# A ring of six tiles with loads of three tiles in a one-core attention decode kernel

## The chip, the core and the metric

The kernel runs on one core of one Trainium2 chip. The metric is the device time of one execution, in microseconds. Five engines matter here: TensorE (PE; its weight loads are shown apart as PEld), VectorE (DVE), ScalarE (ACT), GpSimd (POOL), and SyncE (SP), which in this kernel only issues DMAs, one after the other. The transfers themselves run on 16 DMA engines. "Clock" is the share of its full speed that TensorE was granted.

## The reference

One decode step for four sequences (B = 4, D = 512): adaptive layer norm, attention over a cache with 32 query heads and 8 key/value heads of 4096 keys and 128 channels, and a mixer block over one token. All is fp32.

```python
mod = (silu(c) @ w_mod).reshape(4, 6, 1, -1)
sa, ca, ga, sb, cb, gb = (mod[:, t] for t in range(6))
h = layernorm(x) * (1 + ca) + sa
q = (h @ wq) in 32 heads;  k, v = the caches, each shared by 4 query heads
o = softmax(q k^T * 128 ** -0.5) v
x = x + ga * (o @ wo)
h = layernorm(x) * (1 + cb) + sb
x = x + gb * (gelu(layernorm(h) outer w1 + b1) @ w2 + b2)      # 1792 hidden units
```

The caches are 2 x 32 blocks (4 sequences by 8 heads) of 2 MB each, 128 MB or so of the 157 MB that are read.

## The kernel before

A "head" below is one of the 32 pairs of a sequence and a key/value head, numbered i = 0 to 31 (`NS` = 32). Its keys are a tile of 128 channels by 4096 keys (16 KB in each of 128 partitions), its values one of the same size.

**Buffers.** `ring` has three buffers of 32 KB in each partition, 96 KB in all. A buffer holds two tiles. First it takes the modulation terms 0 and 1 (`wm01`) and the query weights in two halves, then the keys of heads 0 and 1 (`load_first`), then, load by load, K(i+2) and V(i) (`load_pair(i)`), which lie next to each other in HBM, so that one DMA has 128 rows of 32 KB. A buffer is taken again when both of its tiles were read. The modulation terms 2 to 4 (`load_wm24`) pass through a ring buffer too. The output weights, 64 KB in each partition, have tiles of their own (`wo_p`), filled by four DMAs of two heads each (`load_wo`).

**Order.** The program's order is each engine's order (a manual schedule): an engine does its instructions in turn and waits at semaphores. SP holds all loads, so a load that waits for its buffer holds back those behind it.

**A head's work**, in iteration i of the main loop (i = 0 to 23): `scores(i+2)` on PE (L231), the maximum of the scores (DVE, PE), the exponential (ACT, L261), the transposition of the probabilities of head i+1 (DVE, L267), `project(i-1)` with the output weights (PE, L343), and `values(i)` in two halves (PE, L291). So scores run two heads ahead of values. From i = 8 on, a `Mixer` runs beside it for the sequence that is finished: its normalisation, 14 hidden columns (DVE expands, ACT's gelu, PE contracts) and its sum, spread over eight iterations. Behind iteration 2, PE, ACT and DVE work out the modulation terms 2 to 4 (`mod`, L215 and L221).

**The last eight heads** follow an order that is written out (`PLAN`): s is scores, v values, t a transposition, p a projection, x, g and c the mixer's three steps, and LP, LT, LK, LV and LW are loads. The keys of heads 30 and 31 and the values of heads 28 to 31 are loaded on their own, the last values in small pieces, then modulation term 5. Behind the last values comes a serial end: the last projection, the last mixer and the output.

Of the kernel before, what the change touches and what calls it, by code (L numbers as in the profile page):

```python
# [18 lines left out]
P = 128  # L19
# [4 lines left out]
WIDE = {NS - 5: 24, NS - 4: 32}  # L24
NARROW = NS - 3


@with_exitstack
def adaln_decode(ctx: ExitStack, tc: tile.TileContext, small, x, wmod, wq, kk, kv, vv, wo, out):
# [17 lines left out]
    xr = wk.tile([P, D], F32, name="xr", tag="yw", bufs=1)[0:B]  # L47
    wm01 = ring.tile([P, 2, 4, D], F32, name="wm01", tag="kv")
    nc.sync.dma_start(wm01, wmod[0])
    nc.sync.dma_start(sm, small)  # L50
    nc.sync.dma_start(xr, x)
    wqt = []
    for k in range(0, 4, 2):
        t = ring.tile([P, 2, HQ * DH], F32, name=f"wq{k}", tag="kv")
        nc.sync.dma_start(t, wq[k // 2])
        wqt += [t[:, 0], t[:, 1]]
    w1, b1, w2 = sm[:, 0:NF], sm[:, NF:2 * NF], sm[:, 2 * NF:3 * NF]
# [32 lines left out]
    dv.memset(hT, 0.0)  # L90
    wo_p = [wos.tile([P, 2, REP, D], F32, name=f"wo{h}") for h in range(0, HKV, 2)]
    wo_t = [wo_p[h // 2][:, h % 2] for h in range(HKV)]
    prep = cst.tile([P, 4, P], F32, name="prep")
# [62 lines left out]

    KT, VT, WM = {}, {}, {}

    def slots():
        return ring.tile([P, 2, SK], F32, name="kv", tag="kv")  # L160

    def key(t, i):
        KT[i] = t

    def value(t, i):
        VT[i] = t.rearrange("p (j d) -> p j d", d=DH)

    def load_first():
        t = slots()
        nc.sync.dma_start(t, kk)  # L170
        key(t[:, 0], 0)
        key(t[:, 1], 1)

    def load_pair(i):
        t = slots()
        nc.sync.dma_start(t, kv[i])
        key(t[:, 0], i + 2)
        value(t[:, 1], i)

    def load_wo(h):  # L180
        nc.sync.dma_start(wo_p[h // 2], wo[h // 2])

    def load_wm24():
        w = ring.tile([P, 3, 4, D], F32, name="wm24", tag="kv")
        nc.sync.dma_start(w[:, 0:2], wmod[1])
        nc.sync.dma_start(w[:, 2], wmod[2][:, 0])
        for e in range(3):
            WM[2 + e] = w[:, e]

    def load_wm5():  # L190
        t = slots().rearrange("p s (k n) -> p (s k) n", n=D)
        nc.sync.dma_start(t[:, 0:4], wmod[2][:, 1])
        WM[5] = t[:, 0:4]
        return t[:, 4:6]

    def load_key(t, i):
        nc.sync.dma_start(t, kv[i - 2][:, 0])
        key(t, i)

    def load_v(t, i, cuts):  # L200
        value(t, i)
        src = (kv[i][:, 1] if i < NS - 2 else vv[i - NS + 2]).rearrange("p (j d) -> p j d", d=DH)
        for lo, hi in zip(cuts, cuts[1:]):
            nc.sync.dma_start(VT[i][:, lo:hi], src[:, lo:hi])

# [20 lines left out]
    def scores(i):  # L226
        b, h = divmod(i, HKV)
        S[i] = s = ps_s.tile([P, 1024], F32, name=f"s{i}", tag="s")
        for n in range(2):
            for c in range(4):  # L230
                mm(s[32 * c:32 * c + 32, n * 512:(n + 1) * 512], QT[:, b, h, :],  # L231
                   KT[i][:, (n * 4 + c) * 512:(n * 4 + c + 1) * 512], start=True, stop=True)

    def row_max(i):
# [50 lines left out]
    def values(i, ks):  # L285
        if ks[0] == 0:
            PV[i] = ps_v.tile([P, 4 * DH], F32, name="pv", tag="pv")
        pT = PL[i][0]
        for k in ks:
            q = k % 4  # L290
            mm(PV[i][32 * q:32 * q + 32, :], pT[:, 128 * k:128 * k + 128:4],  # L291
               VT[i][:, 4 * k:4 * k + 4, :].rearrange("p j d -> p (j d)"), start=(k < 4), stop=(k >= 4))

    def values_narrow(i, ks, pv=None):
        if ks[0] == 0:
            PV[i] = ps_v.tile([P, DH], F32, name="pvn", tag="pv") if pv is None else pv
        pv = PV[i]
        pT = PL[i][0].rearrange("p (k r) -> p k r", r=32)
        top = 32 if i < NS - 1 else 30
        for k in ks:  # L300
            for j in range(4 * k, min(4 * k + 4, top)):
                c = j % 4
                mm(pv[32 * c:32 * c + 32, :], pT[:, j, :], VT[i][:, j, :], start=(k == 0), stop=(j + 4 >= top))  # L303

    def values_turned(i):
# [31 lines left out]
    def project(i, pa=None, between=None):  # L337
        b, h = divmod(i, HKV)
        oT = OT[i]
        if pa is None:  # L340
            pa = ps_m.tile([P, D], F32, name="pa", tag="m")
            for g in range(REP):
                mm(pa[32 * g:32 * g + 32, :], oT[:, g:g + 1].to_broadcast([P, 32]), wo_t[h][:, g, :],  # L343
                   start=True, stop=True)
        else:
            for g in range(REP):
                for c in range(4):
                    mm(pa[32 * c:32 * c + 32, :], oT[:, g:g + 1].to_broadcast([P, 32]),  # L348
                       wo_t[h][:, g, c * P:(c + 1) * P], start=(g == 0 and h == HKV - 2),
                       stop=(g == REP - 1 and h == HKV - 1))  # L350
                if between and g == 1:
                    between()
# [199 lines left out]
    def finish(b, pg, py, hb, wr):  # L552
        uu = ring.tile([P, 16, D], F32, name="uu", tag="kv")
        for js in ((0,), (1,), (2, 3, 4), (5, 6, 7), (8, 9, 10), (11, 12), (13,)):
# [34 lines left out]
    def fold_gate(gate, es):  # L589
        for e in es:  # L590
            w = wo_t[HKV - 2 + e // REP][:, e % REP]
            dv.tensor_tensor_reduce(w, w, gate, 1.0, 0.0, OP.mult, OP.add, rowsum[:, e:e + 1])
# [15 lines left out]

    load_first()
    load_pair(0)  # L610
    load_wo(0)
    for i in range(2):
# [5 lines left out]
    for i in range(NS - HKV):  # L618
        load_pair(i + 1)
        if i in (1, 3, 5):  # L620
            load_wo(i + 1)
        if i == 1:
            load_wm24()
        scores(i + 2)
# [22 lines left out]
        if mix:  # L647
            mix.outer(i % HKV)
        if i == 2:
            for t in range(2, 5):  # L650
# [4 lines left out]
                else:  # L655
                    nc.scalar.activation(dst, pm, AF.Copy)
        if i == NS - HKV - 2:
            gate = spread_gate()
# [3 lines left out]
    mix, row = Mixer(B - 2), Mixer(B - 1)  # L662
    pve = pgx = pc = ep = spare = slot = None
    gates = list(range(2 * REP))
    cuts = {NS - 1: (0, 16, 24, 28, 30, 32), NS - 2: (0, 16, 32)}
# [3 lines left out]
    x LP27 m26 S27 P24 m27 X26 X27 b26 B26 e26 x b27 v25.1 c g t26.1 l25 t26.0 B27 s28 V25 c g L25  # L669
    v26.0 v26.1 S28 x l26 f a25 L26 V26 A25 x m28 p25 LT X28 e27 c a26 P25 t27.0 A26 b28 s29 f B28 p26 e28  # L670
    LK30 t27.1 S29 P26 v27.0 m29 l27 g LK31 T t28.1 X29 LT t28.0 s30 L27 S30 b29 v27.1 B29 e29 l28 m30 V27
    LV28 L28 a27 g X30 t29.1 t29.0 l29 L29 s31 A27 LV29 b30 p27 x B30 S31 c c m31 e30 P27 X31 v28.0 f LT LV30
    b31 v28.1 B31 f e31 LV31 l30 V28 L30 t30.1 l31 L31 a28 t31.1 A28 p28 v29.0 v29.1 t30.0 f P28 V29 v30.0 a29
    v30.1 A29 LW p29 f v30.2 v30.3 t31.0 P29 g V30 Y y a30 A30 p30 E x v31.0 f v31.1 v31.2 v31.3 V31 z31 a31 I A31 j p31
    g T2 zs za zx zq c c zm zb0 T3 zv zb1 zw0 zn zc
    """
    TABLE = {"s": scores, "S": row_max, "m": turn_max, "X": col_max, "b": spread_max, "B": copy_max, "e": expo,
             "l": sums, "L": scale, "V": copy_v, "a": pick, "A": copy_o, "P": add_up,
             "LP": load_pair}
    MIX = {"F": mix.fold, "R": mix.residual, "G": mix.gather, "M": mix.modulate, "H": mix.gather, "Q": mix.spread,  # L680
# [3 lines left out]
    for step in PLAN.split():  # L684
# [17 lines left out]
        elif op == "p":  # L702
            project(i, pgx[:, 4] if i >= NS - 2 else None, mean_last if i == NS - 1 else None)
        elif op == "LT":
            slot = slots()
        elif op == "LK":
            load_key(slot[:, i % 2], i)
        elif op == "LV":
            load_v(slot[:, i % 2], i, cuts.get(i, (0, 32)))
        elif op == "LW":  # L710
            spare = load_wm5()
        elif op == "x":
            mix.expand(spare if mix.n == 6 else None)
        elif op == "f":
# [74 lines left out]
```

## Time and profile before

| | |
|---|---|
| three runs | 386.31, 386.43 and 390.96 us, median 386.43 |
| profiled execution | span 384.7 us from its first to its last instruction; the page gives no other time of it, and the median of the runs is 1.7 us longer |
| PE, DVE, ACT busy | 78%, 52%, 29% of the span |
| DMA | 7409 packets, 157.69 MB, 410 GB/s over the span |
| mean granted clock | 0.883 |

The span is measured on the core from first to last instruction; the device time also holds what lies around it. A row of the chain of waits gives the share of the span in which an engine, or a DMA, was what the end waited for. A row of instructions has line, engine, operation, output, inputs, shapes and count, then the start and the time; what stands in square brackets is the idle time ahead and what ended it. A window row has the busy times of PE, PEld, DVE, ACT and POOL, then the granted clock, the mean busy share of the DMA engines (which can pass 1 a little, by rounding at the window's edges) and GB/s.

### The profile page before, as it was taken

The page shows a single profiled execution, that of the slowest core. Times are in us where ns is not written, and L with a number is a line of the kernel's source. Part 1 is how long each engine was busy: PE and PEld are TensorE (multiplying, and loading weights), DVE is VectorE, ACT ScalarE, POOL GpSimd, SP SyncE. Part 2 cuts the span into 40 slices and gives each one's busy share as a digit, 9 for nine tenths or more (in the row PEclk, how much of TensorE's full clock was granted, in tenths as well). Part 3 has the DMA queues.
Part 4 walks back from the last instruction along what each step waited for, and adds up shares of the span by engine and source line. Part 5 has one row for each costly group of instructions (what it writes and reads, how often), then busy time and mean ns, then how long its engine had stood idle before and what let it go on. Part 6 is the DMA issues. An engine that isn't in the chain of part 4 may idle for free.

```text
span 384.7 us, 5604 instructions
## 1 busy us (share of the span) xinstructions
PE 298.7 (78%) x2380; PEld 117.2 (30%) x2380; DVE 198.2 (52%) x407; ACT 112.2 (29%) x144; POOL 7.7 (2%) x33
## 2 busy tenths in 40 slices
PE   0856777866966949979877878788888887999984
PEld 0112122311323313334322222342222343333653
DVE  1130251620451424664866545557665567778757
ACT  1001111121110110212567311124575105657276
POOL 1100000000000000000000000000000000000000
PEclk9989555985695685998999998999999999999999
DMA  8999999999999999999999999999999999999930
GB/s 331 433 433 436 411 453 433 409 432 436 423 441 433 434 436 436 434 436 431 429 425 433 428 433 434 429 433 431 429 434 436 434 436 432 424 417 423 418 122 3
DMA packets 7409, 157.69 MB, mean 410 GB/s; under 512 B 964, under 2 KB 1236, under 8 KB 1496
## 3 DMA queue, kind: packets, MB, share of 16 engines
q1 hardware_dynamic: 7376, 157.33, 95.4%
q8 instruction: 18, 0.29, 0.3%
q14 instruction: 7, 0.06, 0.0%
q10 hardware_dynamic: 8, 0.00, 0.0%
HBM read 157.32 MB, written 0.01 MB: 409 GB/s over the span
## 4 chain that ended last, share of the span: by engine, by line
DMA 60%; PE 29%; DVE 7%; ACT 2%; issue 1%; POOL 0%; SPq 0%; POOLq 0%; DVEq 0%
DMA kv<-in_kv 58%; PE s L231 8%; PE pv L291 7%; PE s L122 2%; PE qs L138 2%; DVE m L236 2%; DVE p L267 2%; DMA sm<-in_small 2%; PE pa L343 2%; PE pt L328 2%; ACT uu L562 1%; PE pb L251 1%; PE pve L303 1%; PE pm L240 1%; PE pgx L348 1%
## 5 line engine op out<-in xcount | busy, mean ns | idle before, releaser
L231 PE MATMUL s<-kv,QT 128*32 128x512 f32 x512 | 75.2, 714 | 38.9 <-DMA kv<-in_kv 37.0
L236 DVE TENSOR_REDUCE m<-s 128x1 f32<-128x1024 f32 x32 | 39.2, 1224 | 96.0 <-PE s L231 95.9
L261 ACT ACTIVATE p<-s,nm 128x1024 f32<-128x1024 f32 x32 | 35.7, 1115 | 180.6 <-DVE nm L256 180.5
L291 PE MATMUL pv<-kv,p 128*32 128x512 f32 x464 | 69.8, 670 | 0.7 <-DMA kv<-in_kv 0.7
L231 PEld LDWEIGHTS s<-kv,QT 128*32 128x32 f32 x512 | 15.8, 123 | 84.0 <-DMA kv<-in_kv 52.5
L328 PEld LDWEIGHTS pt<-g,po 128*128 128x128 f32 x236 | 31.1, 205 | 27.2 <-issue 19.9
L343 PE MATMUL pa<-wo,oT 128*32 128x512 f32 x240 | 34.6, 648 | 4.6 <-DVE oT L335 4.4
L328 PE MATMUL pt<-g,po 128*128 128x4 f32 (+2 forms) x236 | 33.9, 267 | 1.5 <-DVE po L314 1.0
L267 DVE STREAM_TRANSPOSE p<-p 128x1024 f32<-128x1024 f32 x25 | 30.9, 1234 | 0.0
L314 DVE COPY po<-pv 128x512 f32<-128x512 f32 x29 | 20.0, 688 | 16.8 <-PE pv L291 16.7
L245 DVE TENSOR_REDUCE mx<-pm 1x128 f32<-1x512 f32 x32 | 21.3, 669 | 1.1 <-PE pm L240 1.1
L442 DVE TENSOR_SCALAR u<-hb,wr,sm 128x512 f32<-128x512 f32 x40 | 19.9, 541 | 1.9 <-POOL wr L437 1.0
L506 ACT ACTIVATE u<-u 128x1024 f32<-128x1024 f32 x20 | 20.4, 1051 | 1.5 <-DVE u L442 1.4
L361 DVE TENSOR_TENSOR acc<-acc,pa 128x512 f32<-128x512 f32 x26 | 17.8, 686 | 4.3 <-PE pa L343 4.2
L261 ACT ACT_TABLE_LOAD x11 | 14.1, 1283 | 20.3 <-DVE nm L256 20.2
L251 PEld LDWEIGHTS pb<-neg,mx 1*128 1x128 f32 x64 | 10.4, 202 | 28.2 <-DVE mx L245 26.5
L122 PE MATMUL s<-wm,sT 128*4 128x512 f32 x16 | 9.1, 732 | 10.6 <-DVE sT L108 10.6
L506 ACT ACT_TABLE_LOAD x13 | 16.7, 1283 | 0.2
L291 PEld LDWEIGHTS pv<-kv,p 128*32 128x32 f32 x464 | 13.4, 146 | 7.2 <-issue 3.1
L240 PE MATMUL pm<-ident,m 128*1 128x128 f32 x32 | 9.3, 289 | 7.4 <-DVE m L236 3.5
L251 PE MATMUL pb<-neg,mx 1*128 1x1 f32 x64 | 13.1, 271 | 2.1 <-DVE mx L245 2.1
L453 PE MATMUL py<-u,sm 128*32 128x512 f32 x80 | 14.4, 616 | 0.0
(158 smaller groups left out, 214.7 us busy)
## 6 DMA issues: line engine op xcount, KB each, us to landing
kv<-in_kv SPq DMA_DIRECT2D x28, 4096.0 KB, 21.9
wq<-in_wq SPq DMA_DIRECT2D x2, 4096.0 KB, 16.3
wo<-in_wo SPq DMA_DIRECT2D x4, 2048.0 KB
kv<-in_kv SPq DMA_DIRECT2D x4, 2048.0 KB, 20.3
wm<-in_wmod SPq DMA_DIRECT2D x2, 2048.0 KB, 14.8
kv<-in_kk SPq DMA_DIRECT2D x1, 4096.0 KB
kv<-in_vv SPq DMA_DIRECT2D x3, 1024.0 KB
wm<-in_wmod SPq DMA_DIRECT2D x1, 1024.0 KB
```

The source lines that it names most:

```text
L231: mm(s[32 * c:32 * c + 32, n * 512:(n + 1) * 512], QT[:, b, h, :], KT[i][:, (n * 4 + c) * 512:(n * 4 + c + 1) * 512], start=True, stop=True)
L236: dv.tensor_reduce(M[i], S[i], axis=AX.X, op=OP.max)
L245: dv.tensor_reduce(mx, M[i].rearrange("o (c r) -> o r c", c=4).unsqueeze(1).to_broadcast([1, 4, 32, 4]), axis=AX.X, op=OP.max)
L251: mm(pb, M[i].rearrange("o c r -> o (c r)"), neg1, start=True, stop=True)
L261: nc.scalar.activation(p, S[i], AF.Exp, bias=M.pop(i), accum_out=l)
L267: dv.transpose(PL[i][0], PL[i][0])
L291: mm(PV[i][32 * q:32 * q + 32, :], pT[:, 128 * k:128 * k + 128:4], VT[i][:, 4 * k:4 * k + 4, :].rearrange("p j d -> p (j d)"), start=(k < ...
L314: dv.tensor_copy(PV[i], pv)
L328: mm(pt, po[:, c * DH:(c + 1) * DH], sel.unsqueeze(1).to_broadcast([P, m, REP]), start=(c == 0), stop=(c == n - 1))
L343: mm(pa[32 * g:32 * g + 32, :], oT[:, g:g + 1].to_broadcast([P, 32]), wo_t[h][:, g, :], start=True, stop=True)
L442: dv.tensor_scalar(u[:, e, :], hb, wr[:, j:j + 1], b1[:, j:j + 1], op0=OP.mult, op1=OP.add)
L506: nc.scalar.activation(u, u, AF.Gelu_apprx_tanh)
```

## The change

- The ring is one tile `RING` of six key or value tiles, again 96 KB in each partition. A list (`queue`) says what is loaded in which order, and `advance` issues the next loads as soon as the tiles that they overwrite have been read in the program's order. It is called behind `scores` and `values`.
- For heads up to 21, a load has three tiles, in rows of 48 KB: K(m+2), V(m), K(m+3), then V(m+1), K(m+4), V(m+2), and so on, 14 loads in all; the host lays the caches out so (`kvk`). Heads after that come in pairs, and the last ones alone, as before; the LP, LT, LK, LV and LW steps of `PLAN` are gone, and its other steps stand as they were.
- Output weights come in two DMAs of four heads. Modulation terms 0 and 1 land in the part of the output weights' tile for heads 0 and 1, and terms 2 to 4, in one DMA, in that for heads 4 to 6, so neither passes through the ring. The output weights are issued when these terms were read.
- The modulation terms 2 to 4 are worked out behind iteration 1, not 2.
- The buffers of the last mixer's hidden columns (`uu`) and of one expansion lie in fixed parts of `RING`.

```diff
-    ring = ctx.enter_context(tc.tile_pool(name="ring", bufs=3))
+    ring = ctx.enter_context(tc.tile_pool(name="ring", bufs=1))
...
+    RING = ring.tile([P, 6, SK], F32, name="kv")
+    wo_t = wos.tile([P, HKV, REP, D], F32, name="wo")
+    wm01, wm24 = wo_t[:, 0:2], wo_t[:, 4:7]
...
+    held, read = [("Q", 0), ("Q", 0), ("Q", 1), ("Q", 1), None, None], {None, ("Q", 0), ("Q", 1)}
...
+    def queue():
+        q = [entry(["K0", "K1"], kk)]
+        for n in range(NT):
+            m = n // 2 * 3
+            names = [f"V{m + 1}", f"K{m + 4}", f"V{m + 2}"] if n % 2 else [f"K{m + 2}", f"V{m}", f"K{m + 3}"]
+            q.append(entry(names, kvk[n]))
+        for i in range(NP, NS - 4):
+            q.append(entry([f"K{i + 2}", f"V{i}"], kv[i - NP]))
...
+        q.append(entry(["W5"], wm5))
+        q.insert(2, ("wo", "M0", wo_t[:, 0:4], wo[0]))
+        q.insert(4, ("wo", None, wm24, wm2))
+        q.insert(6, ("wo", "M2", wo_t[:, 4:8], wo[1]))
+        return q
+
+    LOADS, at = queue(), [4]
+
+    def advance(name=None):
+        read.add(name)
+        while LOADS:
+            kind, names, *rest = LOADS[0]
+            if kind == "wo":
+                if names not in read:
+                    return
+                nc.sync.dma_start(*rest)
+            else:
+                n, p = len(names), at[0]
+                if any(h not in read for h in held[p:p + n]):
+                    return
...
+                held[p:p + n] = names
+                at[0] = (p + n) % 6
...
+                elif len(names) > 1:
+                    nc.sync.dma_start(RING[:, p:p + n], rest[0])
...
+            LOADS.pop(0)
...
     def scores(i):
...
+        advance(f"K{i}")
...
-        if i == 2:
+        if i == 1:
             for t in range(2, 5):
...
+            advance("M2")
...
-    a23 v24.0 A23 p23 t25.0 P23 F R v24.1 LP25 G s26 t25.1 M H V24 LP26 Q a24 S26 v25.0 N s27 x A24 f p24 g
+    a23 v24.0 A23 p23 t25.0 P23 F R v24.1 G s26 t25.1 M H V24 Q a24 S26 v25.0 N s27 x A24 f p24 g
```

SP's loads from the keys of heads 0 and 1 on, before (`in_kk` and `in_kv` are the caches, `in_wo` the output weights, `in_wmod` the modulation terms; a size is partitions by fp32 elements):

```order
L170 DMA kv<-in_kk 128x8192
L176 DMA kv<-in_kv 128x8192
L181 DMA wo_128<-in_wo 128x4096
L176 DMA kv<-in_kv 128x8192 x2
L181 DMA wo_129<-in_wo 128x4096
L185 DMA wm_337<-in_wmod 128x4096
L186 DMA wm_337<-in_wmod 128x2048
L176 DMA kv<-in_kv 128x8192 x2
L181 DMA wo_130<-in_wo 128x4096
L176 DMA kv<-in_kv 128x8192 x2
L181 DMA wo_131<-in_wo 128x4096
L176 DMA kv<-in_kv 128x8192 x21
```

and of the change (`in_kvk` are the loads of three tiles, `in_wm` the modulation terms):

```order
L210 DMA kv<-in_kk 128x8192
L210 DMA kv<-in_kvk 128x12288
L192 DMA wo<-in_wo 128x8192
L210 DMA kv<-in_kvk 128x12288
L192 DMA wo<-in_wm 128x6144
L210 DMA kv<-in_kvk 128x12288
L192 DMA wo<-in_wo 128x8192
L210 DMA kv<-in_kvk 128x12288 x11
L210 DMA kv<-in_kv 128x8192 x7
```

Two big loads of output weights stand where four stood, both among the first six loads, and the second of them stands behind the modulation terms that it overwrites, with all further loads behind it.

PE's work around the modulation terms 2 to 4, before; the rows begin with the second half of head 2's values:

```order
L291 MATMUL pv<-kv,p 32x512 x4
L215 MATMUL pm_445<-wm_337,sT_134 32x512 x4
L221 MATMUL pc_452<-ym,g_122 32x128 x4
L215 MATMUL pm_458<-wm_337,sT_134 32x512 x4
L221 MATMUL pc_465<-ym,g_122 32x128 x4
L215 MATMUL pm_471<-wm_337,sT_134 32x512 x4
L221 MATMUL pc_478<-ym,g_122 32x128 x4
L231 MATMUL s_487<-kv,QT 32x512 x8
```

and of the change, where the rows begin with the second half of head 1's values:

```order
L306 MATMUL pv<-kv,p 32x512 x4
L229 MATMUL pm_380<-wo,sT_129 32x512 x4
L235 MATMUL pc_387<-ym,g_121 32x128 x4
L229 MATMUL pm_393<-wo,sT_129 32x512 x4
L235 MATMUL pc_400<-ym,g_121 32x128 x4
L229 MATMUL pm_406<-wo,sT_129 32x512 x4
L235 MATMUL pc_413<-ym,g_121 32x128 x4
L245 MATMUL s_420<-kv,QT 32x512 x8
```

The scores behind the terms are those of head 5 before and of head 4 now: the three terms moved ahead by one head.

PE's waits in the change, from the scores of head 6 on (s6 to s8 are scores, pv values, pt and pa the projection; a semaphore that begins with DMAHW is that of a load):

```order
L245 MATMUL s6_523<-kv_90,QT_123 32x512 x8
L347 MATMUL pt_535<-g32_121,po_521 128x4 [waits DVE_49]
L347 MATMUL pt_535<-g32_121,po_521 128x4 x3
L290 MATMUL pl_543<-g32_121,l_515 128x4 [waits Activation_49]
L362 MATMUL pa_547<-wo_91,oT_540 32x512 [waits DVE_49]
L362 MATMUL pa_547<-wo_91,oT_540 32x512 x3
L255 MATMUL pm_553<-ident_99,m_533 1x128 [waits DVE_49]
L306 MATMUL pv_557<-kv_90,p_462 32x512 [waits DMAHW4_49]
```

Scores of head 6 came with a load that was waited for earlier, and wait for none; the values of head 4 wait for the load that brings V4, K7 and V5. So PE waits once for each load of three tiles, in turn ahead of scores and ahead of values.

More of the change, by code (lines that the diff above doesn't have):

```diff
@@ L25, with adaln_decode @@
 NARROW = NS - 3
+NT = 14
+NP = NT * 3 // 2
 @with_exitstack
-def adaln_decode(ctx: ExitStack, tc: tile.TileContext, small, x, wmod, wq, kk, kv, vv, wo, out):
+def adaln_decode(ctx: ExitStack, tc: tile.TileContext, small, x, wm0, wm2, wm5, wq, kk, kvk, kv, vv, wo, out):
     nc = tc.nc
     pad = ctx.enter_context(tc.tile_pool(name="pad", bufs=1))
-    ring = ctx.enter_context(tc.tile_pool(name="ring", bufs=3))
+    ring = ctx.enter_context(tc.tile_pool(name="ring", bufs=1))
     wos = ctx.enter_context(tc.tile_pool(name="wos", bufs=1))
@@ L53, in adaln_decode @@
     for k in range(0, 4, 2):
-        t = ring.tile([P, 2, HQ * DH], F32, name=f"wq{k}", tag="kv")
-        nc.sync.dma_start(t, wq[k // 2])
-        wqt += [t[:, 0], t[:, 1]]
+        nc.sync.dma_start(RING[:, k:k + 2], wq[k // 2])
+        wqt += [RING[:, k], RING[:, k + 1]]
     w1, b1, w2 = sm[:, 0:NF], sm[:, NF:2 * NF], sm[:, 2 * NF:3 * NF]
@@ L155, in adaln_decode @@
     nc.scalar.activation(prep[:, 0], px, AF.Copy)
[L157 to L204, printed above, removed]
+    KT, VT, WM = {}, {}, {2 + e: wm24[:, e] for e in range(3)}
+    held, read = [("Q", 0), ("Q", 0), ("Q", 1), ("Q", 1), None, None], {None, ("Q", 0), ("Q", 1)}
@@ new lines, in adaln_decode, with entry @@
+    cuts = {NS - 1: (0, 16, 24, 28, 30, 32), NS - 2: (0, 16, 32)}
+    def entry(names, src):
+        return ("ring", names, src)
+    def queue():
[6 more added lines that the diff above has]
+            q.append(entry([f"K{i + 2}", f"V{i}"], kv[i - NP]))
+        for i in (NS - 2, NS - 1):
+            q.append(entry([f"K{i}"], kv[i - 2 - NP][:, 0]))
+        for i in range(NS - 4, NS):
+            q.append(entry([f"V{i}"], kv[i - NP][:, 1] if i < NS - 2 else vv[i - NS + 2]))
+        q.append(entry(["W5"], wm5))
[3 more added lines that the diff above has]
+        return q
@@ L292, in values @@
                VT[i][:, 4 * k:4 * k + 4, :].rearrange("p j d -> p (j d)"), start=(k < 4), stop=(k >= 4))
+        if ks[-1] == 7:
+            advance(f"V{i}")
     def values_narrow(i, ks, pv=None):
@@ L552, in finish @@
     def finish(b, pg, py, hb, wr):
-        uu = ring.tile([P, 16, D], F32, name="uu", tag="kv")
+        uu = RING[:, 4:6].rearrange("p s (k n) -> p (s k) n", n=D)
         for js in ((0,), (1,), (2, 3, 4), (5, 6, 7), (8, 9, 10), (11, 12), (13,)):
```

79 lines of the change are left out of this document (42 added, 37 removed).

## The prediction

> **What bounds the kernel now.** I read the busy slices first, then the DMA queue and the chain of waits, then windows of the span, then both sides of the ring: PE waiting for DMAs and SP waiting for PE.
>
> ```profile
> PEclk9989555985695685998999998999999999999999
> DMA  8999999999999999999999999999999999999930
> ...
> q1 hardware_dynamic: 7376, 157.33, 95.4%
> ...
> DMA 60%; PE 29%; DVE 7%; ACT 2%; issue 1%; POOL 0%; SPq 0%; POOLq 0%; DVEq 0%
> ```
>
> ```profile
> 0.00:10.00 10.00, 0.00 (x0) 0.00 (x0) 1.42 (x3) 1.50 (x2) 1.75 (x18) 1.00 0.84 322
> 40.00:60.00 20.00, 14.96 (x65) 4.37 (x61) 8.50 (x13) 3.39 (x5) 0.00 (x0) 0.50 1.01 433
> 140.00:160.00 20.00, 16.38 (x92) 6.22 (x96) 7.74 (x13) 1.21 (x2) 0.00 (x0) 0.66 0.99 427
> 260.00:280.00 20.00, 15.39 (x118) 5.63 (x118) 14.42 (x27) 10.79 (x12) 0.00 (x0) 1.00 1.01 435
> ...
> 370.00:384.70 14.70, 8.51 (x172) 5.27 (x172) 10.37 (x27) 10.19 (x14) 0.76 (x2) 0.96 0.01 3
> ```
>
> The DMA share (last column but one of the window rows) is full from the first microseconds to about 367; only the last 15 us run without transfers. The DMA engines are the bound. So a change in the loads can pay in three ways only: fewer bytes (there are none fewer), less cost per packet, or fewer holes; and there are no holes now. It can cost by making holes. The clock in the row PEclk matters because it sets how fast a buffer comes free.
>
> ```profile
> SPq L176 <- PE pv L291: 186.4, 23, 12.3
> ...
> PE s L231 <- DMA kv<-in_kv: 37.0, 19, 6.5
> ...
> kv<-in_kv SPq DMA_DIRECT2D x28, 4096.0 KB, 21.9
> ```
>
> SP waits for the last value matmul of a buffer (L291), issues, and the load lands 21.9 us later.
>
> ```profile
> 251.07 1.92 PE L231 MATMUL s<-kv,QT 128*32 128x512 f32 x16 [1.73 <-DMA kv<-in_kv]
> ...
> 258.74 1.09 PE L291 MATMUL pv<-kv,p 128*32 128x512 f32 x8
> 260.73 1.92 PE L231 MATMUL s<-kv,QT 128*32 128x512 f32 x16 [0.90 <-DMA kv<-in_kv]
> ...
> 265.49 1.09 PE L291 MATMUL pv<-kv,p 128*32 128x512 f32 x8
> ...
> 266.84 1.09 PE L291 MATMUL pv<-kv,p 128*32 128x512 f32 x8
> ...
> 270.39 1.92 PE L231 MATMUL s<-kv,QT 128*32 128x512 f32 x16 [1.60 <-DMA kv<-in_kv]
> ```
>
> Loads of 4096 KB land every 9.66 us (251.07, 260.73, 270.39). So 21.9 is 2.3 periods: about 12 us of work stand ahead of each load when it is issued. That lead is the reserve that the change spends.
>
> **The change part by part.**
>
> *Packets.* Two windows, one of 32 KB rows and one of small rows, give the fixed price of a packet:
>
> ```profile
> DMA packets 849, 24.60 MB, mean 432 GB/s; under 512 B 96, under 2 KB 96, under 8 KB 96
> ...
> q1 hardware_dynamic: 845, 24.54, 99.9%
> ...
> q1 hardware_dynamic: 602, 2.45, 99.5%
> ```
>
> The first is 263 to 320 us: 0.999 x 16 engines x 57 us = 911 engine-us for 845 packets and 24.54 MB. The second is 360 to 366: 95.5 engine-us for 602 packets and 2.45 MB. Solving both gives 9 ns per packet and 36.8 us per MB. Rows saved: 21 heads go from 21 x 128 to 14 x 128 (896 fewer), output weights from 512 to 256, modulation terms from 256 to 128, so 1280. There are ten DMAs fewer, too, each with 16 tiny packets (96 under 512 B in a window of six loads): 160. 1440 x 9 ns / 16 = **0.8 us saved**. A 48 KB row is not in this trace. If it were cut in two, the 21 heads would have 3584 packets instead of 2688, and the saving would turn into a loss of 0.2 us (352 packets more in all). I keep 0.8, since 32 KB rows are uncut and their time per byte agrees with the small rows.
>
> The Trainium skill ("DMA: Bandwidth & Descriptors", section "Anatomy of one DMA — SWDGE (gpsimd) path") gives a DMA a fixed 2.0 us besides its bytes. By that, ten DMAs fewer would bring 20 us; the loads that land every 9.66 us with the engines at 1.01 leave no room for 2 us each, so the trace disagrees for queued loads.
>
> *The start.* Modulation terms 0 and 1 now land in the output weights' tile, so K0 and K1 are issued at once. That hides behind a full queue, and brings nothing.
>
> *Depth of the ring.* The 96 KB are now two loads of 48 KB rows in the first 21 heads. A load takes 1.5 x 9.66 = **14.5 us**. When load n lands, load n+1 is already moving and n+2 must follow within 14.5 us. It may be issued when all three tiles of load n were read. From issue to first data I take 0.9 us:
>
> ```profile
> 0.72 0.39 SPq L49 DMA_DIRECT2D wm<-in_wmod  x1
> ```
>
> (issued at 0.72; the share 0.84 of the first 10 us puts the first data at 1.6). So the reading of a load may take 13.6 us from its landing.
>
> At full clock a head without mixer work takes 260.73 to 267.93 = 7.2 us, of which 2.4 are values (265.49 to 267.93), and a head with the heaviest mixer stage 251.07 to 259.83 = 8.8. A load K, V, K is read in a whole head and the next scores: 7.2 + 1.9 = 9.1 (10.7 with mixer). A load V, K, V takes the values and a whole head: 2.4 + 7.2 = 9.6 (11.2). All are under 13.6: **no hole at full clock**, with 2.4 to 4.5 us to spare.
>
> At a low clock it is near. Bursts that began cold:
>
> ```profile
> 94.58 3.64 PE L231 MATMUL s<-kv,QT 128*32 128x512 f32 x16 [1.72 <-DMA kv<-in_kv]
> ...
> 105.22 1.90 PE L231 MATMUL s<-kv,QT 128*32 128x512 f32 x16
> ...
> 118.86 3.64 PE L231 MATMUL s<-kv,QT 128*32 128x512 f32 x16 [6.45 <-DMA kv<-in_kv]
> ...
> 130.88 1.89 PE L231 MATMUL s<-kv,QT 128*32 128x512 f32 x16
> ...
> 143.25 3.64 PE L231 MATMUL s<-kv,QT 128*32 128x512 f32 x16 [5.20 <-DMA kv<-in_kv]
> ...
> 155.02 1.89 PE L231 MATMUL s<-kv,QT 128*32 128x512 f32 x16
> ```
>
> Scores at half clock take 3.64 instead of 1.92, and these heads took 10.6, 12.0 and 11.8 us: 3.4 to 4.8 more than 7.2. In the changed kernel the idle before a K, V, K load is 14.5 - 9.6 = 4.9 us and before V, K, V 14.5 - 9.1 - 2.8 (from the scores' end to the values) = 2.6, where now it is about 9.66 - 7.2 = 2.5 each time. So cold starts become likelier. A cold K, V, K load takes 9.1 + 4.8 = 13.9, over by 0.3. A cold V, K, V load takes 9.6 + 4.8 = 14.4, over by 0.8; with mixer work 16.0, over by 2.4. The mixer loads wait least, though: 1.5 x 8.8 = 13.2 of 14.5 us are work. I take **one hole of each of the first two kinds, 0.3 + 0.8 = 1.1 us**; the bounds are 0 and, if all five V, K, V loads and all five K, V, K loads that have only one load behind them go over by 2.4 and 0.3, 13.5.
>
> The Trainium skill ("TensorE: Matmul & The Clock Gate", section "What's actually happening") speaks against this change: a whole idle window of about 3.4 us halves the clock. By it all five K, V, K loads would start cold, for holes of 0.3 each: 386.4 - 0.8 + 1.5 = 387.1 instead of 386.7. The trace agrees where the wait was 6.45 and 5.20, yet 94.58 was cold after 1.72, so the wait alone doesn't decide.
>
> *Modulation terms and output weights.* Heads 4 to 7 of the output weights overwrite terms 2 to 4, and may be issued only behind the last product of these. SP runs in order, so the fourth triple stands behind that.
>
> ```profile
> 37.90 2.94 PE L231 MATMUL s<-kv,QT 128*32 128x512 f32 x16 [1.84 <-DMA kv<-in_kk]
> ...
> 82.51 1.47 PE L215 MATMUL pm<-wm,sT 128*32 128x512 f32 x8 [2.49 <-DMA wm<-in_wmod]
> ...
> 89.49 1.94 PE L215 MATMUL pm<-wm,sT 128*32 128x512 f32 x8 [0.40 <-ACT prep L656]
> ...
> 92.21 0.66 PE L221 MATMUL pc<-ym,g 128*32 128x128 f32 x8 [0.78 <-ACT ym L218]
> ```
>
> K0 and K1 land at 37.9. Behind them stand a triple (14.5), 4096 KB of weights (9.7), a triple (14.5) and 3072 KB of terms (7.2): 83.8. The next triple keeps the queue full until 98.3. The products read the terms for 91.43 - 82.51 = 8.9 us, so the weights go out at 92.7, 4.7 us before they must. All steps end at 83.8 + 10.4 = 94.2; then head 2, cold, takes 12.0 at most: 106.2, plus 0.9 is 107.1, and the weights last until 98.3 + 9.7 = 108.0. So this is hidden, by 0.9 us; a longer head would show one for one. PE does head 2 after the terms and not before, and has the time for it: its next load lands only at 98.3.
>
> *The end.* From head 21 on the loads are pairs again, with the order and the small pieces of before, and each of the last tiles comes free on its own, not in twos. The queue is full there anyway. Nothing is gained, and the 17 us behind the last value tile stay.
>
> **Sum.** 384.7 - 0.8 + 1.1 = 385.0 in the profile. The median of the runs shown, 386.43, is 1.7 above its span, so I forecast **386.7**.
>
> **The rivals.**
>
> *No hole at all.* If the clock is high whenever a load lands, or is back within the first scores, only the packets count: 386.4 - 0.8 = 385.6. For it: the last fifteen slices of PEclk are all at 9. Against it: the low clock of the first half, where no mixer fills the waits.
>
> *Holes at each load (slower).* The two buffers leave 13.6 us, PE starts cold each time, and the V, K, V loads with mixer work go over by about 2 us: five of them and 0.3 for each of the other five give 10 + 1.5, so 386.4 - 0.8 + 11.5 = 397.1. It decides from 8.5 us of holes on, which is 2% of the time. For it: the 0.50 and 0.66 of the rows above, and longer waits. Against it: a hole gives PE nothing to wait for, and after a busy head the clock was back (1.89 at 105.22, 130.88, 155.02), so holes don't come twice in a row.
>
> *One tile, so everything waits (the change doesn't do what it says).* If RING were tracked as a whole, each load would wait for the one before: 0.9 us for each of some 30 loads, and 413. The built order speaks against it: scores of a landed key have no wait, and the values behind them wait for one load.
>
> *A small gap per DMA.* The window from 140 to 160 us stands at 0.99: 0.2 us of gaps for two loads, or 0.1 each. Ten DMAs fewer would save 1.0 on top of the packets: 386.4 - 0.8 - 1.0 = 384.6. Against it: the next windows are at 1.00 or over. By the page's 2.0 us each, named above, this rival would come out at 366, for which no row speaks.
>
> **How the numbers follow.** Forecast (holes of 0.3 to 3.5 us: 385.9 to 389.1) 0.60; no hole 0.17; holes beyond that 0.19, of which 0.11 over 2%; one tile 0.02; a gap per DMA 0.02. A measurement here tells about 2% (7.7 us) from no change: faster than 378.7 has 0.01, for the page's price or what I overlook; slower than 394.2 has 0.11 + 0.02 = 0.13, and 0.01 for what I overlook there; the rest is 0.85. The range runs from 385.3 (no hole, and 0.3 of scatter) to 393.0, which leaves out the upper part of the third case and the two small ones, under 2 in 10.
>
> **What would show it.** The queue row should have about 1440 packets fewer at the same 157.3 MB. Windows between 120 and 270 us should show the DMA share at 0.97 or more; under 0.93 the third case holds. SP should wait for scores (L245) at every other triple and for values (L306) at the others, with 5 us to 13 us from landing to issue. Terms 2 to 4 should be read between 84 and 94 us. PEclk should have more low slices before 150 us. I am wrong if the clock stays low through the mixer heads, if 48 KB rows move slower per byte, or if the weights' wait at 107 us runs past the queue.

## The result and the profile after

The change is slower: 396.71 us against 386.44 for the kernel before on the same chip, ratio 1.0241 (95% interval 1.0200 to 1.0282). The forecast was 386.7 with a range to 393.0. Times in this document are medians of all executions, while the ratios leave out slow ones, such as the profiled execution of the change (span 399.9, clock 0.842, the longest of four from 395.36 to 401.74), so its total is not compared below, only its holes. A hole is time in which a DMA engine has nothing to do.

The changed kernel's page, the rows that answer to the ones shown of before:

```profile
PEclk9989558555695959955999899686999999999999
DMA  8999999999999999994999989999899999999930
...
DMA packets 5969, 157.69 MB, mean 394 GB/s; under 512 B 804, under 2 KB 1076, under 8 KB 1336
...
q1 hardware_dynamic: 5936, 157.33, 92.9%
...
DMA 55%; PE 35%; DVE 6%; ACT 2%; issue 1%; SPq 1%; POOL 0%; POOLq 0%; ACTq 0%
...
kv<-in_kvk SPq DMA_DIRECT2D x14, 6144.0 KB, 19.9
```

The packets fell by 7409 - 5969 = 1440, as worked out, at the same bytes. But the DMA row, a line of nines before, has dips (4 in the slice from 180 us, 8 in those from 230 and 280), and the queue's share fell to 92.9%. The engines' time in packets rose by 4.5 us (0.929 x 399.9 = 371.5 us, before 0.954 x 384.7 = 367.0): some packets were slow, as shown further down. The other 10.7 of the 15.2 us that the span gained are time in which the engines had nothing to do.

Windows of the changed kernel (us; busy PE, PEld, DVE, ACT, POOL; clock, DMA share, GB/s):

```profile
100.00:120.00 20.00, 18.33 (x122) 7.12 (x121) 12.28 (x22) 2.41 (x4) 0.00 (x0) 0.83 0.93 385
120.00:140.00 20.00, 11.58 (x71) 3.80 (x71) 5.45 (x10) 2.41 (x4) 0.00 (x0) 0.74 1.01 426
140.00:160.00 20.00, 19.24 (x122) 7.16 (x122) 9.34 (x16) 2.41 (x4) 0.00 (x0) 0.74 0.94 388
160.00:180.00 20.00, 12.08 (x83) 5.35 (x79) 7.81 (x15) 1.21 (x2) 0.00 (x0) 0.71 1.01 433
180.00:200.00 20.00, 19.42 (x126) 8.15 (x122) 11.50 (x25) 5.44 (x7) 1.33 (x3) 0.78 0.69 283
```

Share and PE swing against each other. Where the DMA engines are full (120 to 140, 160 to 180), PE waits and works 12 of 20 us; where PE works 18 to 19 of 20 us, the engines stand for a part of the time (shares 0.93, 0.94, 0.69). The ring no longer lets both run at once.

What SP waited for in the changed kernel (us in total, times, longest):

```profile
SPq L210 <- PE pv L306: 120.0, 12, 13.4
SPq L210 <- PE s L245: 77.3, 7, 16.2
...
SPq L192 <- PE pm L229: 9.5, 1, 9.5
```

and PE:

```profile
PE pv L306 <- DMA kv<-in_kvk: 22.0, 4, 10.1
PE s L245 <- DMA kv<-in_kvk: 21.0, 6, 7.6
```

SP waits for values and for scores in turn, as the prediction said. New is the size of PE's waits: 43.0 / 10 = 4.3 us each, where the 19 of before had 37.0 / 19 = 1.9.

The deepest hole, in the changed kernel's timeline of PE (start, us, instruction, idle before):

```profile
164.91 1.04 PE L306 MATMUL pv<-kv,p 128*32 128x512 f32 x8
173.51 3.64 PE L245 MATMUL s<-kv,QT 128*32 128x512 f32 x16 [7.56 <-DMA kv<-in_kvk]
...
181.48 1.94 PE L306 MATMUL pv<-kv,p 128*32 128x512 f32 x8
...
184.88 1.94 PE L306 MATMUL pv<-kv,p 128*32 128x512 f32 x8
186.60 3.04 PE L245 MATMUL s<-kv,QT 128*32 128x512 f32 x16
```

of SP, which issues the next load as soon as those last scores have been made:

```profile
189.70 0.33 SPq L210 DMA_DIRECT2D kv<-in_kvk  x1
```

and in windows of 1 us (I read shares over 1 as packets whose whole time is put where they start):

```profile
184.00:185.00 1.00, 1.00 (x8) 0.90 (x12) 0.14 (x2) 0.77 (x1) 0.00 (x0) 0.50 0.24 98
185.00:186.00 1.00, 1.00 (x8) 0.29 (x12) 0.69 (x3) 0.43 (x2) 0.57 (x1) 0.50 0.18 66
186.00:187.00 1.00, 1.00 (x8) 0.20 (x4) 0.88 (x4) 0.00 (x0) 0.00 (x0) 0.50 0.00 0
...
189.00:190.00 1.00, 1.00 (x12) 0.44 (x4) 0.29 (x1) 0.00 (x0) 0.00 (x0) 1.00 0.00 0
190.00:191.00 1.00, 0.84 (x8) 0.75 (x7) 1.00 (x3) 0.00 (x0) 0.00 (x0) 1.00 1.90 590
```

K11, V9 and K12 land at 173.5, after PE had idled for 7.56 us. Its scores take 3.64 us (half clock), the values twice 1.94, the next scores end at 189.6: 16.1 us of reading. The load that is moving meanwhile runs out one engine after the other from 184.6 on (at 0.24 and 0.18 only a few still start packets), and the next one is issued at 189.70, when all have stopped. The Trainium skill ("TensorE: Matmul & The Clock Gate", section "What's actually happening") says that a whole idle window of about 3.4 us halves the clock. The half clock behind 7.56 us of idle agrees with it; the length of the window does not come out of this trace: the granted clock fell at 168.4 us, 2.5 us into that wait, and at 250.3 us it fell 0.6 us into another, whose 2.80 us were followed by values at half clock (1.94 us at 252.50).

The last nine loads of three tiles and the first pair behind them, from the trace's records (us; "reading" is from the moment when all 16 engines had landed the load that is overwritten to the issue of the new one; "lead" is from the issue to the moment when the first engine has nothing left; "lost" is by how much the first engine's landing came later than 14.50 us, or 9.68 for the last, after its landing before):

```
issued   overwrites a    reading   first engine   lead    lost
         load landed at            has nothing
137.44      125.38        12.1       138.30        0.9    0.95
153.54      140.34        13.2       153.75        0.2    1.83
166.01      155.98        10.0       170.08        4.1    0.03
189.70      173.47        16.2       184.62       -5.1    6.90
203.54      188.01        15.5       206.02        2.5    0.20
217.18      207.29         9.9       220.72        3.5    0.14
234.75      222.79        12.0       235.36        0.6    1.22
246.87      237.84         9.0       251.08        4.2    0.00
264.91      252.46        12.5       265.57        0.7    1.11
281.04      268.47        12.6       281.18        0.1    1.59
```

With 2.29 for the load issued at 107.51, behind the modulation terms (lead -0.5), 16.3 us are lost. By their times the other three executions lost less, 9.8 to 11.5 us against 385.6 without holes. The last two columns nearly obey one rule: lost = 1.8 - lead, where the lead is under 1.8. The four holes of over 1 us in the run with the terms behind iteration 2 (below) obey it to 0.1 us. (The reading of 15.5 us, most of it at full clock, costs little because the hole ahead of it had made the next landing late as well; PE was still busy with the load before for 1.6 us of it.)

### The profile page after: what moved, and what is told of

It is laid out like the page before. It is cut to its first block, busy times and chain, and to the rows that moved or that the text cites. A ratio compares the mean times of both kernels' runs of the same rounds, so it can differ in the third digit from the quotient of the medians.

```text
span 399.9 us, 5580 instructions
## 1 busy us (share of the span) xinstructions
PE 305.2 (76%) x2380; PEld 121.5 (30%) x2380; DVE 198.4 (50%) x407; ACT 112.2 (28%) x144; POOL 7.7 (2%) x33
## 2 busy tenths in 40 slices
DMA packets 5969, 157.69 MB, mean 394 GB/s; under 512 B 804, under 2 KB 1076, under 8 KB 1336
## 3 DMA queue, kind: packets, MB, share of 16 engines
q1 hardware_dynamic: 5936, 157.33, 92.9%
## 4 chain that ended last, share of the span: by engine, by line
DMA 55%; PE 35%; DVE 6%; ACT 2%; issue 1%; SPq 1%; POOL 0%; POOLq 0%; ACTq 0%
DMA kv<-in_kvk 26%; PE s L245 12%; DMA kv<-in_kv 11%; DMA wo<-in_wm 9%; DMA kv<-in_kk 9%; PE pv L306 8%; PE pa L362 3%; DVE m L251 2%; PE pt L347 2%; DVE p L282 2%; PE pm L229 1%; PE pb L266 1%; PE py L472 1%; ACT kv L581 1%; PE pve L320 1%; PE pm L255 1%
## 5 line engine op out<-in xcount | busy, mean ns | idle before, releaser
L306 PE MATMUL pv<-kv,p 128*32 128x512 f32 x464 | 76.9, 735 | 22.6 <-DMA kv<-in_kvk 22.0
L245 PE MATMUL s<-kv,QT 128*32 128x512 f32 x512 | 74.4, 699 | 25.1 <-DMA kv<-in_kvk 21.0
L347 PEld LDWEIGHTS pt<-g,po 128*128 128x128 f32 x236 | 31.9, 209 | 26.8 <-issue 11.1
L362 PE MATMUL pa<-wo,oT 128*32 128x512 f32 x240 | 35.4, 663 | 4.4 <-DVE oT L354 4.3
L245 PEld LDWEIGHTS s<-kv,QT 128*32 128x32 f32 x512 | 17.5, 125 | 67.2 <-issue 41.4
L347 PE MATMUL pt<-g,po 128*128 128x4 f32 (+2 forms) x236 | 34.7, 271 | 1.5 <-DVE po L333 1.0
L271 DVE COPY nm<-pb 128x1 f32<-128x1 f32 x32 | 5.0, 155 | 43.5 <-PE pb L266 43.4
L306 PEld LDWEIGHTS pv<-kv,p 128*32 128x32 f32 x464 | 13.6, 146 | 29.4 <-DMA kv<-in_kvk 22.8
L266 PEld LDWEIGHTS pb<-neg,mx 1*128 1x128 f32 x64 | 11.4, 221 | 32.4 <-DVE mx L260 24.1
L123 PE MATMUL s<-wo,sT 128*4 128x512 f32 x16 | 9.2, 737 | 10.5 <-DVE sT L109 10.5
L266 PE MATMUL pb<-neg,mx 1*128 1x1 f32 x64 | 14.1, 287 | 2.1 <-DVE mx L260 2.1
## 6 DMA issues: line engine op xcount, KB each, us to landing
kv<-in_kv SPq DMA_DIRECT2D x7, 4096.0 KB, 16.3
```

What stands on the lines that cost most here:

```text
L266: mm(pb, M[i].rearrange("o c r -> o (c r)"), neg1, start=True, stop=True)
L347: mm(pt, po[:, c * DH:(c + 1) * DH], sel.unsqueeze(1).to_broadcast([P, m, REP]), start=(c == 0), stop=(c == n - 1))
```

## The experiments

My theory after the result: a ring of two loads cannot be read in time, because a load counts as landed only as a whole, and each late issue leaves the DMA engines dry. Rivals: rows of 48 KB move badly; the new place of the output weights and terms starts a series of holes; the low clock alone makes them; the mixer's work alone makes them. Each ratio is against the kernel before on the same chip.

**Loads of two tiles in the new ring** (all else of the change is kept, but the second weights stand one place later):

```diff
-NT = 14
+NT = 0
...
-        for n in range(NT):
-            ...
-        q.insert(6, ("wo", "M2", wo_t[:, 4:8], wo[1]))
+        q.insert(7, ("wo", "M2", wo_t[:, 4:8], wo[1]))
```

> The changed kernel with all heads in loads of two tiles (three loads fit the ring of six tiles); output weights in two loads, terms two to four in one, and the ring as one tile stay. If the loss is holes from a ring of only two loads: no holes, and 432 packets fewer than in the kernel before, at 9 ns each on 16 engines 0.2 us: 386.2. If the loss is in the other parts (weights behind the terms, terms one head earlier, one tile): 390 or more. If nothing but noise: near 396 as the change.

386.54 us against 386.51, ratio 0.9998 (0.9989 to 1.0007). Its page:

```profile
DMA  8999999999999999999999999999999999999700
...
q1 hardware_dynamic: 6944, 157.33, 94.0%
...
kv<-in_kv SPq DMA_DIRECT2D x28, 4096.0 KB, 21.7
```

No hole. The single tile `RING`, the two weight loads, the one load of terms and the earlier products cost nothing together. The loss sits in the loads of three tiles. (This page is of the longest of its runs, with a span of 389.8 us: its caches have landed at 367.6, before the change at 367.5, and what it is longer by lies behind that.) That 432 packets fewer bring 432 x 9 ns / 16 = 0.24 us could not be seen.

**Three DMAs of one tile where the change has one of three**, at the same place and behind the same wait (the pairs are split as well):

```diff
-                    nc.sync.dma_start(RING[:, p:p + n], rest[0])
+                    for k in range(n):
+                        nc.sync.dma_start(RING[:, p + k], rest[0][:, k])
```

> The changed kernel with each load of three tiles issued as three DMAs of one tile, at the same place and behind the same waits. If it is the landing of a whole load that delays its reading: PE reads the first tile 9.7 us earlier, only the hole of about 2.3 us behind the terms is left, and 4032 packets more cost 2.3 us: 390. If what matters is that three tiles must all be read before any is loaded again: the holes stay, 396 + 2 = 398. If rows of 48 KB were slow by themselves: 388 or less, with no holes in the DMA share.

388.01 us, ratio 1.0039 (1.0026 to 1.0053). Its windows:

```profile
100.00:150.00 50.00, 41.15 (x310) 14.94 (x310) 26.78 (x48) 7.23 (x12) 0.00 (x0) 0.97 1.01 432
150.00:200.00 50.00, 39.93 (x315) 16.67 (x311) 31.38 (x61) 18.62 (x22) 1.33 (x3) 1.00 1.01 430
200.00:250.00 50.00, 39.51 (x298) 14.88 (x298) 27.88 (x56) 11.45 (x15) 0.55 (x1) 0.93 1.01 429
```

No hole, with the buffers, the order and even the issuing condition of the change. What differs is that the tile which is read first lands 9.7 us before the last, so the reading begins, and ends, that much sooner. The hole behind the terms is gone as well: the weights go out at 94.53 and the next tile at 94.91. The time alone fits the third case too, that rows of 48 KB were slow; the next run keeps the short rows and decides.

**The same three DMAs in reversed order**, so that the tile that PE needs first lands last:

```diff
+                    for k in reversed(range(n)) if n == 3 else range(n):
+                        nc.sync.dma_start(RING[:, p + k], rest[0][:, k])
```

> As the kernel with three DMAs of one tile for each load of three, but the three are issued in reverse, so the tile that PE needs first lands last. If it is the wait for the whole load that makes the holes, they are back: the change's 396.7 and about 2 us for packets, 398 to 399. If short rows or more DMAs are what cures: 388.

398.39 us, ratio 1.0296 (1.0245 to 1.0348). Its windows:

```profile
150.00:200.00 50.00, 38.06 (x259) 15.21 (x259) 26.00 (x53) 12.72 (x17) 1.33 (x3) 0.86 0.98 408
200.00:250.00 50.00, 40.62 (x278) 15.21 (x278) 25.50 (x45) 16.14 (x18) 0.00 (x0) 0.83 0.91 372
```

The DMAs, packets and rows of 16 KB of the run before; only the waiting for all three tiles is back, and with it the holes. This pair is the decisive one: the loss is the landing as a whole, and neither the length of a row nor the number of DMAs.

**Single tiles, each loaded when its own place is free:**

```diff
-            q.append(entry(names, kvk[n]))
+            for k, nm in enumerate(names):
+                q.append(entry([nm], kvk[n][:, k]))
...
-        q.insert(2, ("wo", "M0", wo_t[:, 0:4], wo[0]))
-        q.insert(4, ("wo", None, wm24, wm2))
-        q.insert(6, ("wo", "M2", wo_t[:, 4:8], wo[1]))
+        q.insert(4, ("wo", "M0", wo_t[:, 0:4], wo[0]))
+        q.insert(8, ("wo", None, wm24, wm2))
+        q.insert(12, ("wo", "M2", wo_t[:, 4:8], wo[1]))
```

> The changed kernel with the same tiles in the same order and places, each of the 42 tiles of the first 21 heads loaded by a DMA of its own as soon as its own tile was read. Holes from the ring's depth: none left, packets cost 2.3 us more than in the change: 386.4 - 0.8 + 2.3 = 387.9. If the loss came from the order of the tiles or the weights' place: 396 or more.

387.61 us, ratio 1.0027 (1.0013 to 1.0040). This has 10002 packets, 4033 more than the change, and the split run 11154, 5185 more. From the no-hole case of the prediction (385.6) at 9 ns each they come to 385.6 + 2.3 = 387.9 and 385.6 + 2.9 = 388.5; measured 387.6 and 388.0. So the sum with the price of a packet holds to half a microsecond, and a ring that is fed tile by tile pays nothing else that shows. Against the kernel before, whose 7409 packets these exceed by 2593 and 3745, they cost 1.1 and 1.5 us, 6 to 7 ns for each packet.

**The terms behind iteration 2 again, the second weights one place later:**

```diff
-        q.insert(6, ("wo", "M2", wo_t[:, 4:8], wo[1]))
+        q.insert(7, ("wo", "M2", wo_t[:, 4:8], wo[1]))
...
-        if i == 1:
+        if i == 2:
```

> The changed kernel with the terms two to four worked out behind iteration 2 again, and the second load of output weights one place later, behind the fourth load of three tiles. This takes away the first hole (at 107 us in the change), of 2.3 us with its restart. If each hole stands for itself: 396.7 - 2.3 = 394.4. If one hole lowers the clock and so makes the next: 391 or less. If that hole doesn't count: 396.7.

398.21 us, ratio 1.0322 (1.0268 to 1.0375). SP's timeline in this run:

```profile
89.62 0.33 SPq L210 DMA_DIRECT2D kv<-in_kvk  x1
```

The load that the change issues at 107.51 goes out at 89.62 and lands in its step of 14.50, so the first hole is gone. The time isn't better: other holes came, of 1.3, 4.9, 2.8 and 2.5 us for the loads issued at 164.78, 198.66, 230.30 and 261.78. That hole didn't start the series; two of the three cases of the expectation had the time fall, and it didn't.

**The kernel before with two buffers of 32 KB instead of three:**

```diff
-    ring = ctx.enter_context(tc.tile_pool(name="ring", bufs=3))
+    ring = ctx.enter_context(tc.tile_pool(name="ring", bufs=2))
```

> The kernel before with two ring buffers in place of three, rows of 32 KB as before, so two loads of two tiles. If the depth in loads is what counts: a load must be read within 9.7 us less a restart of about 1.7 us, heads take 7.2 to 12 us, and each hole costs up to 4 us per two loads: 400 to 430. If 48 KB rows are the cause: near 386.5.

438.74 us, ratio 1.1268 (1.1193 to 1.1343). Its windows:

```profile
200.00:250.00 50.00, 41.07 (x259) 14.90 (x262) 26.11 (x49) 19.92 (x21) 0.00 (x0) 0.79 0.84 348
250.00:300.00 50.00, 38.69 (x240) 15.69 (x232) 22.14 (x45) 7.84 (x11) 1.30 (x3) 0.75 0.82 335
```

The same pattern without a row of 48 KB: two loads in the ring, shares under 0.9, a low clock. The depth counts in loads that land as a whole. The time lies above the 400 to 430 expected. Some 6 us of the loss come ahead of the heads: the first keys reach the ring at 42.8 us instead of 36.9, as the query weights before them pass through the two buffers as well.

**Idle matmuls to keep the clock up.** `warm(n)` makes n matmuls of 512 columns into a PSUM tile that nobody reads. First 12 ahead of the scores and 8 ahead of the values that wait:

```diff
+        if i % 3 == 0 and 3 <= i < 22:
+            warm(12)
...
+        if i % 3 == 1 and 3 <= i < 22:
+            warm(8)
```

> The changed kernel with idle matmuls on PE into a spare tile ahead of each wait for a load of three tiles (12 ahead of scores, 8 ahead of values, heads 3 to 21), so that the clock stays high. If the holes come from the low clock: only the hole behind the terms is left, 386.4 - 0.8 + 2.3 = 388, with the granted clock over 0.9. If two loads are too few at any clock: 396 or more, as the added work delays the reading by up to 2.9 us.

397.94 us, ratio 1.0274 (1.0228 to 1.0320). The clock rose to 0.904 only, and the deepest hole still lay behind a stretch at half clock:

```profile
170.00:180.00 10.00, 10.00 (x48) 4.13 (x46) 4.04 (x7) 0.21 (x1) 0.00 (x0) 0.54 0.97 418
180.00:190.00 10.00, 9.24 (x61) 3.39 (x65) 5.92 (x12) 0.99 (x2) 0.57 (x1) 0.78 0.66 251
```

So this one tells nothing of the clock. With 20 and 10 of them, on top of the run with the terms behind iteration 2:

```diff
+        if i % 3 == 0 and 3 <= i < 22:
+            warm(20)
...
+        if i % 3 == 1 and 3 <= i < 22:
+            warm(10)
...
-        if i == 1:
+        if i == 2:
```

> The change with the terms behind iteration 2 and the weights one place later, and with 20 idle matmuls on PE ahead of a wait for scores and 10 ahead of a wait for values (heads 3 to 21). If the low clock is the cause of the holes: 389 or less with the clock at 0.93 or more. If two loads are too few at the full clock too, or the idle work itself delays the reading: 394 or more.

398.08 us, ratio 1.0274 (1.0211 to 1.0338). Its windows:

```profile
141.00:161.00 20.00, 18.57 (x148) 7.51 (x144) 11.74 (x21) 2.41 (x4) 0.00 (x0) 1.00 1.01 432
161.00:181.00 20.00, 18.85 (x163) 7.58 (x167) 12.52 (x27) 2.41 (x4) 0.57 (x1) 1.00 0.99 409
...
221.00:243.00 22.00, 20.09 (x172) 7.25 (x171) 11.85 (x23) 3.67 (x5) 0.00 (x0) 1.00 0.97 400
```

Now the clock is full from 141 to 243, and holes remain: five of the six loads issued from 163.94 to 240.27 lost 0.8 to 1.1 us each, for readings of 10.8 to 12.2 us. Leads of 1.2 to 1.9 us lost 0.3 to 0.9 us more here than 1.8 less the lead, so the rule of the table gives too little for this run. The largest loss of this run, 2.5 us, is outside that stretch, at the load issued at 257.91, behind a reading of 13.4 us. A full clock alone doesn't cure the mixer's heads. (Idle matmuls that still ran when a load landed may hold a part of these readings.)

**The same without the mixer of the first two sequences** (two tiles that it would have filled are set to zero at the start):

```diff
-        if i and i % HKV == 0:
-            mix = Mixer(i // HKV - 1)
```

> The kernel with the terms behind iteration 2 and idle matmuls ahead of the waits, and without the mixer of the first two sequences (left out: their normalisation, hidden columns and sums; the output of these two sequences isn't computed). Heads then take 7.2 us at the full clock, a load of three tiles 9.1 to 9.6 from its landing. If a load must be read within about 10 us of its landing, no hole is left: 386 to 387.5. If two loads of 48 KB rows lose a restart each time whatever the reading takes: 394 or more.

391.47 us, ratio 1.0113 (1.0089 to 1.0137). Its windows:

```profile
130.00:150.00 20.00, 16.22 (x109) 5.30 (x101) 5.43 (x9) 1.20 (x2) 0.00 (x0) 0.74 1.00 431
150.00:170.00 20.00, 18.89 (x146) 6.92 (x142) 9.21 (x16) 2.41 (x4) 0.00 (x0) 0.91 0.92 365
...
210.00:230.00 20.00, 18.13 (x146) 6.16 (x146) 8.74 (x16) 2.41 (x4) 0.00 (x0) 1.00 1.01 432
230.00:250.00 20.00, 18.49 (x149) 7.33 (x149) 9.85 (x17) 2.41 (x4) 0.00 (x0) 1.00 1.00 431
```

At full clock and without mixer work the readings are 9.0 to 10.1 us, and the six loads issued from 180.34 to 254.64 lose 0.2 each on average, 0.5 at most. The two holes of 2.0 and 2.2 us at 150.51 and 167.34 fall behind readings of 12.5 and 14.7 us with stretches at half clock in them. So the time lies between the two cases of the expectation, and these two cold readings cost 4.1 of the some 5 us that its loads of three tiles lost.

**Without that mixer, and without idle matmuls** (the run with the terms behind iteration 2 and this edit):

```diff
-        if i and i % HKV == 0:
-            mix = Mixer(i // HKV - 1)
```

> As that kernel (the mixer of the first two sequences left out), but without the idle matmuls, so PE idles longer and its clock falls. If the low clock alone can make holes: 391 to 396, with the clock well under 0.9. If only the mixer's work in the heads made them: 386 to 387.5, as with the idle matmuls.

396.65 us, ratio 1.0260 (1.0240 to 1.0280), clock 0.839. Its windows:

```profile
150.00:170.00 20.00, 15.68 (x100) 4.86 (x100) 8.09 (x15) 2.41 (x4) 0.00 (x0) 0.83 0.97 394
...
210.00:230.00 20.00, 13.30 (x90) 4.93 (x90) 9.21 (x16) 2.41 (x4) 0.00 (x0) 0.83 0.96 397
250.00:270.00 20.00, 15.54 (x96) 5.73 (x88) 7.92 (x14) 1.78 (x4) 0.00 (x0) 0.76 0.97 399
```

With less work PE waits longer, its clock falls, and the holes are back. The clock is worth 396.65 - 391.47 = 5.2 us here. So either of the two, low clock or mixer work, suffices to pass the limit. No version beat the kernel before; the nearest, loads of two tiles, equals it.

## Why the prediction was wrong

- **The bound** (right). The DMA engines bound the kernel, and the change could only pay in packets or cost in holes.
- **Packets** (right). 1440 fewer; 48 KB rows are uncut (1792 of them in the trace, 14 x 128) and a load of three tiles lands 14.50 us after the one before where nothing delays it, against 14.5 worked out. The gain of 0.8 us cannot be shown on its own, but the runs with single tiles bear out the size of the price.
- **The reading of a load** (right in size). Forecast 9.1 and 9.6 us at full clock without mixer: measured 9.0 to 10.1. With mixer 10.7 and 11.2: 10.1 to 12.2 for most in the run at full clock. Cold 13.9 to 16.0: 12.0 to 13.2 and once 16.2.
- **"So the reading of a load may take 13.6 us from its landing"** (the step that failed). By this rule two of the ten readings of the table are too long, by 16.2 - 13.6 = 2.6 us and 15.5 - 13.6 = 1.9 us; the ten gave 14.0. Two terms were too small. First, load n+1 doesn't run for 14.5 us behind the landing of load n that PE sees. PE waits for the last of the 16 engines, which in the change finishes 1.3 to 3.4 us behind the first (184.62 and 188.01 for the load above), and the first then runs out that much earlier. Before, the engines lay as far apart, but with 5 us of lead or more at every load it cost nothing. Second, an issue to engines that have nothing left costs 1.8 us and not 0.9. A load takes 16.3 us from the issue at 189.70 to the first landing at 206.02, against 14.50 in a stream. First packets come after 0.96 us, as I took it from the kernel's start, but are slow: in the row from 190 to 191 us, 590 GB/s are 12 rows of 48 KB, and 1.90 x 16 / 12 makes 2.5 us for each. In the steady stretch behind it, with the changed kernel's queue row for 208 to 219 us,

```profile
q1 hardware_dynamic: 97, 4.77, 100.7%
```

  a row takes 1.007 x 16 x 11 / 97 = 1.83 us. From the landing of load n to the moment when the first engine has nothing left, the table has 11.2 to 13.4 us in eight of its ten rows (more in the two rows behind the longest holes), where the prediction had 14.5. Less 1.8 us, from 9.4 (ahead of the issue at 189.70) to 11.6 us are left for the reading. The 2.4 to 4.5 us "to spare" at full clock shrink to between 2.5 and less than nothing, and loads with mixer work can go over at full clock, as the run with idle matmuls showed.
- **"A hole gives PE nothing to wait for … so holes don't come twice in a row"** (wrong). A hole makes the next landing late, PE idles, and the clock falls for the reading that follows: 7.56 us of idle ahead of the reading of 16.2. I had used this sentence to hold the case of holes at each load at 0.19. That its 397.1 is near the measured 396.7 is partly luck: the holes came at loads of both kinds and were of 1 to 7 us, where it had five of about 2 and five of 0.3.
- **Modulation terms and weights** (wrong by 3.2 us: a cover of 0.9 was forecast, and a hole of 2.3 came). The terms were read from 84.9 to 94.3, and the weights went out at 94.34 (forecast 92.7). The next load of three tiles went out at 107.51, 1.3 us later than forecast (106.2); the first engine had run out at 107.0, 1.0 earlier than forecast (108.0); and the restart took 0.9 more. But taking the hole away didn't shorten the kernel.
- **One tile that makes all wait** (rightly put aside): loads of two tiles in `RING` run as before. **A gap per DMA** (rightly put aside): 36 DMAs more in the split run cost no more than their packets.

Left open: how the loss divides between clock and mixer at each load, since each moves the other; and why the first packets behind an empty queue are slow.

## What to carry to other kernels

Count a ring's depth in landings, not in bytes: a consumer that waits for a whole load starts late by all of it, and two loads in the ring leave less than one load's time to read the other. Before making loads larger, list for each load how long before the queue runs dry its issue comes (here 5 us and more before the change, 0.1 to 4.2 and below zero in it), and keep some 3 us to the moment when the first DMA engine runs out (leads of 2.4 to 2.7 us still lost 0.1 to 0.5 in these runs). If larger rows are wanted, let each tile be waited for on its own: the split run did with the change's ring what one DMA of three tiles could not.

## What was not expected of the hardware

- The 16 DMA engines drift apart within one stream, and a load's end is spread over 0.8 us at the start (37 us), and later over 1.7 to 3.4 before the change and 1.3 to 3.4 after it. It is hidden until something waits for the whole load with little lead.
- A restart of an empty queue costs 1.8 us in all. The Trainium skill ("DMA: Bandwidth & Descriptors", section "Anatomy of one DMA — SWDGE (gpsimd) path") gives about 2.0 us as the fixed price of one DMA on another issuing path. This trace has a price near that only where the queue had run dry; queued loads followed each other every 14.50 us with none.
- Clock and transfers feed back: with less PE work (no mixer) the time stayed at 396.65 with the clock at 0.839, and more of it (idle matmuls) brought 391.47 with 0.916.
